# Loading one weight in five pieces to move the last store to the last semaphore of the closing list

## Chip, cores, metric

The kernel runs on one core of one Trainium2 chip. The metric is device time in microseconds (us); a median of several executions is quoted. All runs here were in the fast state with the full TensorE clock (granted clock 1.0 in every run whose clock is listed). The engines are named as in the profile: PE (TensorE; PEld is its weight loads), DVE (VectorE), ACT (ScalarE), POOL (GpSimd), SP (SyncE, which here issues every DMA).

## The reference

Two layers, each a sliding dilated attention block A and a gated MLP block B, with residuals. S = 2048 tokens, D = 1024, F = 3584, 32 heads, bfloat16.

```python
def _A_ref(x, wqkv, wo):        # q, k, v = x @ wqkv; 8 keys per token, 2 apart; softmax
    ...
    return o.reshape(B, S, D) @ wo

def _B_ref(x, w1, w3, w2):
    h = silu(x @ w1) * (x @ w3)
    return h @ w2

x = x + _A_ref(_layernorm(x), A_wqkv, A_wo)
x = x + _B_ref(_layernorm(x), B_w1, B_w3, B_w2)
x = x + _A_ref(_layernorm(x), A_wqkv, A_wo)
x = x + _B_ref(_layernorm(x), B_w1, B_w3, B_w2)
```

## The kernel before

The kernel records every operation with its reads and writes in a list, places the list with its own scheduler, and emits it in that order. The framework under it supplies the semaphores. Each DMA goes through one helper, and `wo` (2 MB) is one DMA, loaded once, in the first stage:

```python
def dma(kb, dst, src, reads, writes, cls=3, transpose=False):
    def emit(op):
        ...
        nc.sync.dma_start(dst, src)
    return pr.add("SP", 0.45, emit, reads, writes, cls, size=kb * 1024)

# ... end of q_first(), the first stage
dma(2048, wo[:], wo_v, [("d", 0, 2, 0, 6)], ["wo"], 3)

# ... t_stage(): the matmuls that use it
op = mm8(a, [(oT[oh][:, t, j * P:(j + 1) * P], wo[:, t, hh * 512:(hh + 1) * 512]) for t in range(KT)],
         True, True, [("oT", oh, t) for t in range(KT)] + ["wo"], lane=1)

# ... b_stage(): the last result leaves in small pieces
evac(dve, ..., nc.vector.tensor_tensor(xs, xs, bank[a.bank][:, 0:cn], op=ALU.add), ...)
if l == 1:
    dma(cn // 4, xout[:, n, ...], xs, [("x", n, hh)], [("out", n, hh)], 0)

# ... the emission
with tc.manual_schedule():
    for op in pr.place():
        op.emit(op)
```

The framework deals the DMAs to eight semaphores, 0 to 7, in turn. It also closes the program: SP waits for every semaphore's final value, two semaphores to an instruction, in a fixed order, and then all engines meet twice. SP's closing part, as built (numbers are DMA semaphores; DVE and ACT stand for the semaphores on which these engines report):

```
wait (3, 2)   wait (4, 1)   wait (5, 0)   wait (6, DVE)   wait (7, ACT)
drain, waits for POOL
drain, reports to POOL       wait for POOL's release     (first meeting)
drain, reports to POOL       wait for POOL's release     (second meeting)
```

Before has 468 DMAs, so the last store is on semaphore 3: the first of the five waits.

Of the kernel before, what the change touches and what calls it, by code (L numbers as in the profile page):

```python
# [154 lines left out]
def kernel(  # L155
# [15 lines left out]
    KT = D // P  # L171
# [16 lines left out]
    wo_v = A_wo.rearrange("(i t) n -> i t n", t=KT)  # L188
# [9 lines left out]
    def alloc(name, shape, dt=BF16):  # L198
        return sb.tile(shape, dt, name=name)
# [14 lines left out]
    wo = alloc("wo", [P, KT, D])  # L214
# [20 lines left out]
    oT = [alloc(f"oT{i}", [P, KT, TCH]) for i in range(2)]  # L235
# [8 lines left out]
    def t1(n):  # L244
        return 0.15 + n / 960.0
# [7 lines left out]
    def dma(kb, dst, src, reads, writes, cls=3, transpose=False):  # L253
        def emit(op):
            if transpose:
                nc.sync.dma_start_transpose(dst, src)
            else:
                nc.sync.dma_start(dst, src)  # L258
        return pr.add("SP", 0.45, emit, reads, writes, cls, size=kb * 1024)
# [77 lines left out]
    def mm8(a, pairs, first, last, reads, lane=0, ncol=512, takes=True):  # L337
        n = len(pairs)

        def emit(op):  # L340
            for i, (w, r) in enumerate(pairs):
                nc.tensor.matmul(bank[a.bank][:, 0:ncol], lhsT=w, rhs=r, start=first and i == 0,  # L342
                                 stop=last and i == n - 1)
        return pr.add("PE", n * (ncol / 2400.0 + 0.0025), emit, reads, [], takes=[a], lane=lane, lag=0.17)

    def evac(add, dur, emit, last_mm, reads, writes, a, cls=0, **kw):
        op = add(dur, emit, reads, writes, cls, gives=[a], **kw)
        op.deps.add(last_mm)
        return op
# [39 lines left out]
    def q_tile(l, c, which, ws, b, keep=None):  # L389
        for m0 in range(0, KT, 2):  # L390
            i = n_sgt[0] % 4
            n_sgt[0] += 1
            for m in (m0, m0 + 1):
                a = Acc()
                lk = [q_lhs(ws, kk, m) for kk in range(KT)]
                op = mm8(a, [(w, xnT[b][:, kk, :]) for kk, (w, _) in enumerate(lk)], True, True,
                         list({k for _, k in lk}) + [("xnT", b, j) for j in range(TPC)])
                evac(act, 0.59, lambda _, a=a, i=i, m=m: nc.scalar.copy(sgt[i][:, m % 2, :], bank[a.bank][:]), op, [],  # L398
                     [("sgt", i, m % 2)], a)
                if keep:  # L400
                    evac(act, 0.4, lambda _, a=a, m=m: nc.scalar.copy(keep[1][:, m, HALO:], bank[a.bank][:, 0:TCH]),
                         op, [], [(keep[0], m)], a)
            dma(256, spill_view(l, which, m0, c, ws[1] == "s"), sgt[i][:], [("sgt", i, 0), ("sgt", i, 1)],
                [("d", l, which, c, m0)], 1)
# [28 lines left out]
    def q_first():  # L433
# [86 lines left out]
        for which, key, tile_ in ((1, "kT", kT), (2, "vT", vT)):  # L520
            dve(0.11, lambda _, tile_=tile_: nc.vector.memset(tile_[:, :, 0:HALO], 0.0), [], [(key, "h")], 1)
            q_tile(0, 0, which, wslots[which], b, (key, tile_))
        dma(2048, wo[:], wo_v, [("d", 0, 2, 0, 6)], ["wo"], 3)
        stage_no[0] += 1

    def allkeys(key):
# [23 lines left out]
    def t_stage(l, half):  # L550
# [46 lines left out]
        oh = half % 2  # L597
# [7 lines left out]
        for j in range(TCH // P):  # L605
            n = tok0 // P + j
            for hh in range(2):
                a = Acc()
                op = mm8(a, [(oT[oh][:, t, j * P:(j + 1) * P], wo[:, t, hh * 512:(hh + 1) * 512]) for t in range(KT)],
                         True, True, [("oT", oh, t) for t in range(KT)] + ["wo"], lane=1)  # L610
                xs = x_sb[n][:, hh * 512:(hh + 1) * 512]
                evac(dve, t1(512), lambda _, xs=xs, a=a: nc.vector.tensor_tensor(xs, xs, bank[a.bank][:], op=ALU.add),  # L612
                     op, [("x", n, hh)], [("x", n, hh)], a)
# [72 lines left out]
    def attend(l, c):  # L686
        for r in range(R):
            t_stage(l, c * R + r)

    q_first()  # L690
    attend(0, 0)
    for c in range(1, NCH):
# [47 lines left out]
```

## Time and profile before

| | before |
|---|---|
| device time, first three runs | 1616.17 us median (1616.09 to 1616.46) |
| span of the profiled run | 1613.4 us |
| end of the last matmul to end of span | 2899 ns |
| issue of the last store to end of span, called **the tail** below | 2544 ns |
| SP's records in the trace | 845 |

The page shows what bounds the kernel. The rows with digits give busy tenths in 40 equal slices.

```profile
span 1613.4 us, 19212 instructions
...
PE 1608.5 (100%) x7610; PEld 762.2 (47%) x7610; DVE 1122.8 (70%) x1908; ACT 327.0 (20%) x521; POOL 5.0 (0%) x28
...
PE   9999999999999999999999999999999999999999
...
PEclk9999999999999999999999999999999999999999
```

PE is busy from end to end at full clock. The chain of work that ended last says the same in order of time. Its columns are start, length and what it was, all in us:

```profile
21 pieces in order of time: start us, us, what
...
1.66 2.78 DMA x<-in_A_x_dram
...
14.84 6.99 PE bank L504 x64
21.83 1588.68 PE bank L342 x7416
1610.51 0.02 issue
1610.54 0.29 DVE x L667
```

From 14.84 us on the chain is PE alone, for 1595.67 us. What a change can shorten without touching the matmuls is the start before that, and the end after 1610.51. The timeline of the end shows the last VectorE add, then the last store's issue on SP, and then no engine's work until 1613.4:

```profile
1610.54 0.29 DVE L667 TENSOR_TENSOR x<-x,bank 128x128 bf16<-128x128 bf16 x1 [1.28 <-PE bank L342]
1610.85 0.33 SPq L258 DMA_DIRECT2D out_dram<-x  x1
```

The waits and drains of the closing part are not counted as work and do not show there. The view of the launch line (the line of kernel.py that starts the program; the framework's closing instructions are put down to it) groups them for SP: count, duration in ns as min/median/max, first and last start in us.

```profile
L735 SPq EVENT_SEMAPHORE  x7: 17/28/28, 1612.3 to 1613.3; - x7
L735 SPq DRAIN  x3: 7/7/7, 1612.6 to 1613.0; - x3
```

One by one they are records of the trace. Below are SP's last eleven: its record number, start in ns before the end of the span, duration, and the gap since SP's record before it ended (this listing is worked out from the trace's records and is no view of the profile):

```
before
row   start   took   gap
835   -2544    332   1172   issue of the last store (semaphore 3)
836   -1069     28   1143   wait (3, 2)
837   -1005     28     36   wait (4, 1)
838    -943     28     34   wait (5, 0)
839    -879     28     36   wait (6, DVE)
840    -818     28     33   wait (7, ACT)
841    -753      7     37   drain
842    -689      7     57   drain, reports        first meeting
843    -537     17    145   wait for release
844    -445      7     75   drain, reports        second meeting
845     -63     17    375   wait for release
```

The store lands and ends the wait (3, 2) 1475 ns after its issue. The trace has the last update of semaphore 3 at 1086 ns, and the record of its wait starts 17 ns later. Four waits that were satisfied long ago are then worked off, 63 ns apart (61 to 64): 1069 - 818 = 251 ns on the critical path.

Last, the wo load before: one issue of 2 MB, 9.6 us from issue to landing.

```profile
L258 SPq DMA_DIRECT2D wo<-in_A_wo_dram x1: 497/497/497, 56.9 to 56.9; - x1
...
DMA to landing us min/median/max: 9.6/9.6/9.6
```

### The profile page before, as it was taken

To read this page: it belongs to the slowest core of one execution; us is meant where nothing else is said; L and a number is where in the kernel's file an instruction comes from. 1 tells how busy PE (TensorE), PEld (TensorE's weight loads), DVE (VectorE), ACT (ScalarE), POOL (GpSimd) and SP (SyncE) were. 2 spreads that over 40 slices of the span, in tenths; PEclk is the share of its full clock that TensorE was granted. 3 is DMA by queue.
4 is the path that set the end of the run, shared out by engine and by line. 5 is a ranking of instruction groups with operands and counts; after the bars stand their busy time and mean duration, and the time that the engine had idled before them with its cause. 6 is when DMAs were issued, how large, how long until landed. Compare 5 with 4: busy or idle time off the path is not lost.

```text
span 1613.4 us, 19212 instructions
## 1 busy us (share of the span) xinstructions
PE 1608.5 (100%) x7610; PEld 762.2 (47%) x7610; DVE 1122.8 (70%) x1908; ACT 327.0 (20%) x521; POOL 5.0 (0%) x28
## 2 busy tenths in 40 slices
PE   9999999999999999999999999999999999999999
PEld 7555544444444444444444444444444444444444
DVE  6898888889888888988888819884289831211211
ACT  4423322021201222113211032110321101101110
POOL 1000000000000000000000000000000000000000
PEclk9999999999999999999999999999999999999999
DMA  9834755485548764858554488355873464454451
GB/s 316 233 105 151 220 167 171 131 213 167 171 143 249 195 186 135 217 165 251 175 163 133 156 234 243 120 176 175 253 221 118 160 179 156 144 178 149 156 168 41
DMA packets 350073, 285.80 MB, mean 177 GB/s; under 512 B 72224, under 2 KB 344864, under 8 KB 349856
## 3 DMA queue, kind: packets, MB, share of 16 engines
q1 hardware_dynamic: 349984, 284.59, 58.7%
q8 instruction: 59, 0.97, 0.2%
q14 instruction: 30, 0.25, 0.1%
HBM read 238.94 MB, written 29.36 MB: 166 GB/s over the span
## 4 chain that ended last, share of the span: by engine, by line
PE 99%; DMA 0%; ACT 0%; SPq 0%; DVE 0%; issue 0%; ACTq 0%
PE bank L342 98%; PE bank L490 0%; PE bank L504 0%; DMA x<-in_A_x_dram 0%; PE bank L419 0%; ACT xn L453 0%; SPq L258 0%; DVE xn L457 0%; DVE x L667 0%; ACTq L453 0%
## 5 line engine op out<-in xcount | busy, mean ns | idle before, releaser
L342 PE MATMUL bank<-xnT,slot 128*128 128x512 bf16 x5056 | 1094.2, 379 | 0.0
L342 PEld LDWEIGHTS <-slot 128*128 128x128 bf16 x5056 | 517.9, 102 | 573.2
L342 PE MATMUL bank<-slot,hT 128*128 128x512 bf16 (+2 forms) x1848 | 389.2, 373 | 0.0
L637 DVE TENSOR_TENSOR hT<-sg,bank 128x512 bf16<-128x512 bf16 x224 | 153.1, 684 | 213.3 <-PE bank L342 201.5
L262 DVE TENSOR_TENSOR scr<-scr 128x1024 bf16<-128x1024 bf16 (+3 forms) x576 | 291.8, 535 | 2.0
L342 PEld LDWEIGHTS <-hT 128*128 128x128 bf16 x1848 | 178.4, 98 | 208.8
L635 ACT ACTIVATE sg<-bank 128x512 bf16<-128x512 f32 x224 | 133.7, 597 | 662.2 <-PE bank L342 624.9
L262 DVE TENSOR_TENSOR scr<-qT,kT 128x2048 bf16<-128x2048 bf16 x128 | 153.8, 1216 | 75.1 <-DMA kT<-qkv_d 73.5
L398 ACT CAST sgt<-bank 128x512 bf16<-128x512 f32 x184 | 107.4, 585 | 351.4 <-PE bank L342 348.7
L262 DVE TENSOR_TENSOR scr<-pA,vT 128x2048 bf16<-128x2048 bf16 x128 | 152.0, 1216 | 0.3
L667 DVE TENSOR_TENSOR x<-x,bank 128x512 bf16<-128x512 bf16 (+1 forms) x66 | 43.8, 670 | 123.5 <-PE bank L342 123.5
L342 PE MATMUL bank<-wo,oT 128*128 128x512 bf16 x512 | 113.1, 379 | 0.0
L309 DVE BATCH_NORM_STATS2 st<-x 128x6 f32<-128x512 bf16 x128 | 84.2, 680 | 10.7 <-DMA x<-in_A_x_dram 10.4
L342 PEld LDWEIGHTS <-oT 128*128 128x128 bf16 x512 | 50.1, 98 | 60.3
L612 DVE TENSOR_TENSOR x<-x,bank 128x512 bf16<-128x512 bf16 x64 | 43.8, 685 | 31.5 <-PE bank L342 30.5
L595 DVE STREAM_TRANSPOSE pA<-pB 128x2048 bf16<-128x2048 bf16 x16 | 37.0, 2311 | 0.5
L572 DVE STREAM_TRANSPOSE pB<-pA 128x2048 bf16<-128x2048 bf16 x16 | 37.0, 2310 | 0.4
L262 DVE TENSOR_TENSOR pA<-scr 128x256 bf16<-128x256 bf16 x128 | 35.4, 282 | 0.4
L323 DVE TENSOR_SCALAR xn<-x,mv,rstd 128x1024 bf16<-128x1024 bf16 x64 | 31.9, 540 | 4.1 <-DMA xnT<-xn 3.7
L316 ACT ACTIVATE sd<-mv,epst 128x4 f32<-128x4 f32 (+1 forms) x19 | 5.7, 299 | 142.5 <-DVE mv L312 142.3
L635 ACT ACT_TABLE_LOAD x19 | 24.4, 1283 | 48.4 <-PE bank L342 48.3
L262 DVE TENSOR_TENSOR oT<-scr 128x256 bf16<-128x256 bf16 x128 | 33.4, 282 | 0.1
(55 smaller groups left out, 203.6 us busy)
## 6 DMA issues: line engine op xcount, KB each, us to landing
slot<-in_B_w_dram SPq DMA_DIRECT2D x160, 1024.0 KB, 6.3
slot<-in_A_wqkv_dram SPq DMA_DIRECT2D x28, 1024.0 KB, 5.1
qkv_d<-sgt SPq DMA_DIRECT2D x92, 256.0 KB, 3.8
qT<-qkv_d SPq DMA_DIRECT2D x16, 512.0 KB, 4.8
slot<-in_B_w_dram SPq DMA_DIRECT2D x16, 512.0 KB, 5.8
kT<-qkv_d SPq DMA_DIRECT2D x14, 544.0 KB, 5.8
vT<-qkv_d SPq DMA_DIRECT2D x14, 544.0 KB, 5.5
out_dram<-x SPq DMA_DIRECT2D x31, 128.0 KB, 4.1
```

What stands on the lines that cost most here:

```text
L262: return lambda _: nc.vector.tensor_tensor(o, a, b, op=op)
L309: dve(0.67, lambda _, hh=hh: nc.vector.bn_stats(st[q][:, j, hh, :], x_sb[n][:, hh * 512:(hh + 1) * 512]), [("x", n, hh)] + list(after), [( ...
L316: act(0.3, lambda _: nc.scalar.activation(sd[q][:, j0:j1], mv[q][:, j0:j1, 1], ACTF.Sqrt, bias=epst[:]), [("mv", q, j) for j in range(j0, ...
L323: dve(0.5, lambda _: nc.vector.tensor_scalar(xn[j][:], x_sb[n][:], mv[q][:, j, 0:1], rstd[q][:, j:j + 1], op0=ALU.subtract, op1=ALU.mult), ...
L342: nc.tensor.matmul(bank[a.bank][:, 0:ncol], lhsT=w, rhs=r, start=first and i == 0, stop=last and i == n - 1)
L398: evac(act, 0.59, lambda _, a=a, i=i, m=m: nc.scalar.copy(sgt[i][:, m % 2, :], bank[a.bank][:]), op, [], [("sgt", i, m % 2)], a)
L572: dve(2.31, lambda _: nc.vector.transpose(psmT[:].rearrange("p c d -> p (c d)"), psm[:].rearrange("p w s -> p (w s)")), allA, ["pB"])
L595: dve(2.31, lambda _: nc.vector.transpose(At[:].rearrange("p w s -> p (w s)"), AeT[:].rearrange("p c d -> p (c d)")), ["pB"], allA)
L612: evac(dve, t1(512), lambda _, xs=xs, a=a: nc.vector.tensor_tensor(xs, xs, bank[a.bank][:], op=ALU.add), op, [("x", n, hh)], [("x", n, hh) ...
L635: evac(act, 0.6, lambda _, i=i, a=ag: nc.scalar.activation(sg[i][:], bank[a.bank][:], ACTF.Silu), og, [], [("sg", i)], ag, table="silu")
L637: evac(dve, t1(512), lambda _, i=i, a=au, f=f: nc.vector.tensor_tensor(hT[:, f, :], sg[i][:], bank[a.bank][:], op=ALU.mult), ou, [("sg", i ...
L667: evac(dve, t1(cn), lambda _, xs=xs, a=a, cn=cn: nc.vector.tensor_tensor(xs, xs, bank[a.bank][:, 0:cn], op=ALU.add), op, [("x", n, hh)], [ ...
```

## The change

The intent: four more DMAs make 472, so the last store falls on semaphore 7, whose wait is the last of the five. The four others are then worked off while the store is in flight.

```diff
-        dma(2048, wo[:], wo_v, [("d", 0, 2, 0, 6)], ["wo"], 3)
+        for t0, t1_ in ((0, 2), (2, 4), (4, 6), (6, 7), (7, 8)):
+            dma(256 * (t1_ - t0), wo[:, t0:t1_, :], wo_v[:, t0:t1_, :], [("d", 0, 2, 0, 6)], [("wo", t0)], 3)
...
-                         True, True, [("oT", oh, t) for t in range(KT)] + ["wo"], lane=1)
+                         True, True, [("oT", oh, t) for t in range(KT)] + [("wo", t) for t in (0, 2, 4, 6, 7)], lane=1)
```

## The prediction

> **What bounds the kernel now.** TensorE, from the first microseconds to the last. The page gives PE busy 1608.5 us of a 1613.4 us span, the full clock in all 40 slices, and a chain that ended last of which 98% is one matmul line. The trace's matmul records show no gap over 20 ns after 6.3 us. DVE is at 70%, ACT at 20%, the DMA queue at 58.7%. So only the two ends can become shorter: the first 6 us, and the 2.9 us from the last matmul's end (1610.50) to the end of the span.
>
> **The tail, from the trace's raw records** (ns before the end of the span). The last VectorE add starts at 2861 and takes 289; the last store is issued at 2544; its last packet starts at 1456; the wait that it ends passes at 1069. Then SyncE steps through the rest of its closing list at 63 ns each: 1005, 943, 879, 818 (four more paired waits), 753 and 689 (two drains), then two rounds of the all-engine barrier to the end. The list takes the eight DMA semaphores in fixed order, (3,2), (4,1), (5,0), (6,DVE), (7,ACT). DMAs are dealt to the semaphores in turn. Before has 468, so the last store is on semaphore 3, the first wait of the list, and four satisfied waits are worked off after the landing.
>
> **What the change does.**
> - It removes nothing and adds four DMA issues. 472 DMAs put the last store on semaphore 7, the last wait; the other four then pass while the store is in flight. Worth 1069 - 818 = 251 ns, all on the critical path. [...] here 387 ns lie between last packet and wait. That part stays.
> - The four issues cost at most 0.5 us each of SyncE (the 2 MB one takes 497 ns) near 57 us of the timeline, where SyncE mostly waits for ScalarE. The wo load lands at about 66.5 us; its first matmul is at 106.3 us. The spill buffers form a ring of four, each filled in about 3.5 us of matmuls, so a spill issued 2 us late does not reach PE.
> - Built, the programs have the same instruction order on PE, DVE, ACT and POOL and the same number of standalone waits; on SyncE only the wo pieces differ.
>
> **Prediction.** 1616.17 - 0.25 = 1615.92 us, 0.016% faster, less than the spread of the three runs (0.37 us). Eight times in ten between 1615.55 and 1616.30. Faster by over 2%: 0.003; within 2%: 0.994; slower by over 2%: 0.003.
>
> **What would show each step.** Span about 1613.15. The wait for semaphore 7 passes about 1475 ns after the last store's start, as that for semaphore 3 did; those for 3 to 6 lie before it; from it to the end 0.82 us instead of 1.07. No PE gap after 6.3 us; last matmul's end at 1610.5 within 0.05. Five wo issues, landed before 80 us.
>
> **What would make it wrong.** The last store's landing varies by over 0.25 us between runs; a wait that has blocked costs more after its release than a satisfied one; late spills near 57 us do stall PE (a gap of up to 2 us there); or the time outside the span (1.8 us in the profiled run) moves by as much.

No term of the sum is cut: it came to 1616.17 - 0.25 = 1615.92 us, and the 0.25 is the 251 ns between two starts in the listing of before. That such starts may be differenced, the prediction did not show; for the wait (3, 2) the 17 ns between the semaphore's last update and the record's start show it.

## The result, and the profile after

| | before | after |
|---|---|---|
| median | 1616.07 us (1615.23 to 1616.46, 6 runs) | 1615.88 us (1615.14 to 1616.00, 6 runs) |
| ratio of the fast runs | | 0.9999, 95% interval 0.9986 to 1.0012 |
| span of the profiled run | 1613.4 us | 1614.2 us |
| end of the last matmul | 1610.50 us | 1611.36 us |
| end of the last matmul to end of span | 2899 ns | 2808 ns |
| tail | 2544 ns | 2454 ns |
| SP's records | 845 | 849 |

A ratio here and below is the mean time of one kernel's fast runs over that of the other's of the same rounds, so not quite the ratio of the medians quoted. The median landed beside the predicted 1615.92 us. But the profile doesn't show the predicted parts. The span of this one profiled run is longer by 0.8 us, and the tail is shorter by only 90 ns instead of 251.

The 0.8 us lie at the start. The page and the chain of after:

```profile
span 1614.2 us, 19216 instructions
...
PE 1609.6 (100%) x7610; PEld 762.0 (47%) x7610; DVE 1123.4 (70%) x1908; ACT 327.1 (20%) x521; POOL 5.0 (0%) x28
...
PE   9999999999999999999999999999999999999999
```

```profile
26 pieces in order of time: start us, us, what
...
4.50 5.72 DMA slot<-in_A_wqkv_dram
...
15.70 6.99 PE bank L504 x64
22.69 1588.68 PE bank L342 x7416
1611.37 0.02 issue
1611.40 0.29 DVE x L668
```

The last 7416 matmuls take 1588.68 us in both kernels, to the hundredth. Only the point at which they begin differs, 21.83 against 22.69 us: in this run a load of the first weights landed at 10.22 us and was waited for, where before the x loads and the first transposes set the pace. The changed DMAs are issued at 57 us, so the change has no part in it. The span scatters from run to run in both kernels: after's six runs go from 1613.4 to 1614.2 us, and nine runs of before, taken later on one chip, from 1613.6 to 1614.4. The profiles put this scatter at the start: in the six that have all PE records, the row of 7416 matmuls takes 1588.68 or 1588.69 us and begins anywhere from 21.83 to 23.54 us.

The five pieces of wo were issued by 61.5 us (60.6 + 0.9) and landed within 7.6 us each:

```profile
L258 SPq DMA_DIRECT2D wo<-in_A_wo_dram x5: 339/478/882, 57.8 to 60.6; - x5
...
DMA to landing us min/median/max: 5.4/7.2/7.6
```

The end. First the view of the launch line for SP; one drain now takes 130 ns instead of 7, and the first wait starts already at 1612.1:

```profile
L736 SPq EVENT_SEMAPHORE  x7: 17/28/28, 1612.1 to 1614.1; - x7
L736 SPq DRAIN  x3: 7/7/130, 1613.2 to 1613.8; - x3
```

The same records one by one, listed as for before:

```
after
row   start   took   gap
839   -2454    332   1169   issue of the last store (semaphore 7)
840   -2076     28     46   wait (3, 2)
841   -2012     27     36   wait (4, 1)
842   -1950     28     35   wait (5, 0)
843   -1886     28     36   wait (6, DVE)
844    -996     28    862   wait (7, ACT)
845    -920      7     48   drain
846    -871      7     42   drain, reports        first meeting
847    -719     17    145   wait for release
848    -339    130    363   drain, reports        second meeting
849     -63     17    146   wait for release
```

The intended part worked. Four waits pass while the store is in flight, the wait on semaphore 7 passes 1458 ns after the issue (1475 before), and the first drain that reports comes 125 ns after it, where before it took 380. But from that drain to the end SP takes 871 ns where it took 689. The 182 ns are lost at one place: row 848 starts 363 ns after row 847 (75 ns before the change), and takes 130 ns (7 before). POOL waits for that report. Counted back from the end, its own clean-up before the second meeting was done at 409 ns, SP's report ended at 209, and POOL's wait passed at 183. Before the change SP's report had ended at 438 and POOL's clean-up at 228, so the report had about 210 ns in hand; that is why a report 411 ns late costs 182. In all the tail is 17 (the landing) + 255 - 182 = 90 ns shorter.

### What is special about row 848

In SP's records of before, a pause of 0.35 us or more stands in front of rows 80, 208, 336, 464, 592 and 720: 80 plus multiples of 128. After has it at the same row numbers, although other instructions stand there now. The gap in ns before each of these rows:

```
row        80   208   336    464   592   720   848
before    447  3250   369   5286  1156   354   (ends at row 845)
after     452   360   354  11656  5198   359   363
```

Some of these gaps include a wait. Over the ten traces there are 68 such rows, and not one gap is under 331 ns; the median gap over all other rows is about 51 ns. No other place in the count of 128 behaves so: at each of the other 127 places the shortest gap is at most 53 ns. The next in the series is 848. Before ends three records short of it. After has four records more, and so the change itself carried SP's program over it, on the last report, the last instruction but one of SP's program.

What the pause is was not shown. The page lists two queues with packets of the kind "instruction": in after 59 on queue 8, of 16384 bytes in the trace, and 31 on queue 14, of 8192. The first on queue 14 after row 847 starts 1.03 us after it (0.99 to 1.26 us in the eight profiles that reach row 848). In after that is 0.67 us after row 848 itself has started, so SP did not pause for that packet. No run here changes these packets. The pause itself and its place are measured.

### The profile page after: what moved, and what is told of

Same layout as the page of the kernel before. It is cut to its first block, busy times and chain, and to the rows that moved or that the text cites. A ratio compares the mean times of both kernels' runs of the same rounds, so it can differ in the third digit from the quotient of the medians.

```text
span 1614.2 us, 19216 instructions
## 1 busy us (share of the span) xinstructions
PE 1609.6 (100%) x7610; PEld 762.0 (47%) x7610; DVE 1123.4 (70%) x1908; ACT 327.1 (20%) x521; POOL 5.0 (0%) x28
## 4 chain that ended last, share of the span: by engine, by line
PE 99%; DMA 0%; SPq 0%; issue 0%; DVE 0%
PE bank L342 98%; PE bank L504 0%; DMA slot<-in_A_wqkv_dram 0%; PE bank L490 0%; SPq L258 0%; PE bank L419 0%; DVE x L668 0%
```

## The experiments

Theory F: a pause of about 0.3 us stands at every 128th SP record; the four added issues move it onto the closing drain, and that gives back 182 of the 251 ns. Rival C: the slow drain was an accident of one run. A second rival ties it to the split load, or to the last store being on the last semaphore. The first four kernels ran on one chip, the other four on another, each group beside nine runs of before on the same chip. Their tails were read from one profile each. In the profiles of e1 to e4 about 150 records of PE are missing; SP's are complete (row counts as built).

| run | last store on | SP rows | row 848 is | tail expected by F | tail measured | median, us | before, same chip |
|---|---|---|---|---|---|---|---|
| before | 3 | 845 | not reached | | 2544 | 1616.07 | |
| after | 7 | 849 | drain, second meeting | | 2454 | 1615.88 | 1616.07 |
| e1_after_again | 7 | 849 | drain, second meeting | 2454 | 2464 | 1615.88 | 1615.91 |
| e2_after_pad8 | 7 | 857 | first closing wait | 2272 | 2294 | 1615.85 | 1615.91 |
| e3_before_pad4 | 3 | 849 | drain, second meeting | 2726 | 2759 | 1616.23 | 1615.91 |
| e4_after_pad3 | 7 | 852 | drain right after the landing | 2580 | 2706 | 1616.21 | 1615.91 |
| e5_pieces4 | 6 | 848 | last wait of all | 2357 | 2335 | 1615.47 | 1615.93 |
| e6_pieces6 | 0 | 850 | wait, first meeting | 2420 | 2449 | 1616.01 | 1615.93 |
| e7_pieces8 | 2 | 852 | drain right after the landing | 2966 | 2998 | 1616.26 | 1615.93 |
| e8_merge4 | 7 | 838 | not reached | 2294 | 2276 | 1615.69 | 1615.93 |

All results were correct, and every time ratio to before lies between 0.9998 and 1.0002 with an interval of about 0.13% on either side, so no single time proves a difference. The tails do: the only program profiled twice (after, and e1) differs by 10 ns, and the part of the tail that hangs on the store's landing, from the last store's issue to the pass of its wait, lies between 1458 and 1478 ns in the eight profiles where the record shows it directly (all but e6 and e7).

### e1_after_again

Edit: none.

> The changed kernel, unaltered, to see what repeats. Tail = from the issue of the last store to the end of the span: 2544 ns before, 2454 ns after, in the two profiles so far. Theory F [...]: SyncE pauses about 0.31 us at every 128th of its instructions; the four added DMA issues put such a pause on its second closing drain (row 848 of 849), which gives back 182 of the 251 ns. Then the tail repeats: 2454 +- 40 ns, with about 360 ns before row 848. Rival C (chance): the slow drain was an accident of one run; then the tail is about 2290 ns. Time: 1615.9 us for F, 1615.8 for C; the start of the kernel scatters by about 0.8 us in either.

Measured: tail 2464 ns, with gap 363 and 130 ns for row 848 again, to the nanosecond as in after. Rival C falls.

### e2_after_pad8

Empty drains on SP, in mid-kernel where SP mostly waits for other engines (984 us of before's span for PE alone), are there only to shift row numbers:

```diff
+n_sp = 0
 for op in pr.place():
     op.emit(op)
+    if op.eng == "SP":
+        n_sp += 1
+        if n_sp == 300:
+            for _ in range(8):
+                nc.sync.drain(fusable=False)
```

> After, with 8 empty drains on SyncE in mid-kernel: same DMAs, same semaphores, 857 SyncE rows, so row 848 becomes the first of the closing waits, which is passed while the last store is still in flight. F: the pause is hidden, tail 2272 +- 40 ns (251 + about 20 below before), median about 1615.7 us. Rival C or a rival that ties the slow drain to the split load or to the last semaphore: tail as in after, 2454 ns.

Measured: tail 2294 ns, 160 to 170 ns below after's two profiles. The view of the launch line shows the drain short again:

```profile
L742 SPq EVENT_SEMAPHORE  x7: 17/28/28, 1611.7 to 1613.2; - x7
L742 SPq DRAIN  x3: 7/7/7, 1612.6 to 1612.9; - x3
```

The pause is still there, 343 ns in front of row 848, but that row is now the first closing wait, and the store is still in flight. From the wait on semaphore 7 to the end it takes 818 ns, exactly as from the same wait in before. So 251 ns is what the semaphore's place is worth when nothing takes it back.

### e3_before_pad4

Edit: the same insertion with 4 drains, in the kernel before (one wo load, last store on semaphore 3).

> Before, with 4 empty drains on SyncE in mid-kernel: one wo load, last store on semaphore 3, but 849 SyncE rows as in after. F: row 848 is again the second closing drain; tail 2544 + 182 = 2726 +- 40 ns, median about 1616.25 us. Rivals (chance, split load, last semaphore): 2544 ns, 1616.07 us.

Measured: tail 2759 ns, 215 above before.

```profile
L741 SPq EVENT_SEMAPHORE  x7: 17/28/28, 1613.2 to 1614.4; - x7
L741 SPq DRAIN  x3: 7/7/116, 1613.5 to 1614.1; - x3
```

The slow drain appears without a split load and without the last semaphore, by the row count alone (gap 382, 116 ns). This disposes of the second rival.

### e4_after_pad3

Edit: the same insertion with 3 drains, in after.

> After, with 3 empty drains: 852 rows, so row 848 is the drain that directly follows the wait for the last store. F: the pause lies wholly on the critical path: tail 2272 + 310 = 2580 +- 50 ns, worse than before's 2544 although the last store is on the last semaphore; median about 1616.0 us. Rivals: 2454 ns (split load or last semaphore), 2290 ns (chance).

Measured: tail 2706 ns, so worse than before, as F said, but by more than its 2580 ± 50.

```profile
L742 SPq EVENT_SEMAPHORE  x7: 17/28/28, 1612.1 to 1614.4; - x7
L742 SPq DRAIN  x3: 7/7/130, 1613.6 to 1614.0; - x3
```

The size was off, not the place. I had taken the pause as the gap alone, 0.31 us. Where row 848 is a drain, the drain itself also takes 130 ns instead of 7. From the wait on semaphore 7 to the report it takes 551 ns here (1240 - 689) and 129 in e2 (818 - 689), so the pause costs 422 ns where nothing hides it. The expectations of the next group use that.

### e5_pieces4

```diff
-for t0, t1_ in ((0, 2), (2, 4), (4, 6), (6, 7), (7, 8)):
+for t0, t1_ in ((0, 2), (2, 4), (4, 6), (6, 8)):
```

with the list of keys that the matmuls read changed alike (so also in the next two).

> After, with wo in four pieces instead of five: 471 DMAs, last store on semaphore 6, so one satisfied wait is left behind it (63 ns); 848 SyncE rows, so the pause falls before the very last wait, in front of which SyncE idles 375 ns anyway. F: tail 2294 + 63 = 2357 +- 40 ns, about 100 ns below the five pieces although the last store is not on the last semaphore. If only the semaphore's place counted: 63 ns above the five pieces, 2525 ns. Median about 1615.8 us.

Measured: tail 2335 ns, below after's although the last store is not on the last semaphore. Row 848 is the very last wait; its gap is 376 ns, as it was at that place in before without any pause (375), so the pause hides there for free.

### e6_pieces6

```diff
-for t0, t1_ in ((0, 2), (2, 4), (4, 6), (6, 7), (7, 8)):
+for t0, t1_ in ((0, 2), (2, 4), (4, 5), (5, 6), (6, 7), (7, 8)):
```

> wo in six pieces: 473 DMAs, last store on semaphore 0, two satisfied waits behind it (126 ns); 850 rows, row 848 is SyncE's wait for the first barrier's release. There SyncE idles 145 ns, so it is late by about 210 ns, within the about 230 ns that the second drain has in hand (its 411 ns delay in after cost 182). F: tail 2294 + 126 = 2420 +- 50 ns. If only the semaphore's place counted: 126 ns above the five pieces, 2590 ns.

Measured: tail 2449 ns. The wait at row 848 came 374 ns after the row before it instead of 145, and most of that was absorbed by the slack of the second meeting: the tail is 29 ns above the 2420 that two satisfied waits alone give. The median was above before's although the tail is shorter by 95 ns; the profiled run began its long row of matmuls at 23.54 us, 1.71 us later than that of before, so this run carries the start's scatter.

### e7_pieces8

```diff
-for t0, t1_ in ((0, 2), (2, 4), (4, 6), (6, 7), (7, 8)):
+for t0, t1_ in ((0, 1), (1, 2), (2, 3), (3, 4), (4, 5), (5, 6), (6, 7), (7, 8)):
```

> wo in eight pieces: 475 DMAs, last store on semaphore 2, in the first closing wait as in before, so no gain from the semaphore; 852 rows, so row 848 is the drain behind the wait for the last store, which cost 422 ns in full with the three pads. F: tail 2544 + 422 = 2966 +- 50 ns, the slowest of all, median about 1616.45 us. If only the semaphore's place counted: 2544 ns, as before.

Measured: tail 2998 ns, the longest of all, 454 above before, at a place in the closing list that is no worse than before's.

```profile
L736 SPq EVENT_SEMAPHORE  x7: 17/28/1112, 1611.9 to 1614.4; - x7
L736 SPq DRAIN  x3: 7/7/130, 1613.6 to 1614.0; - x3
```

A side finding sits in the first line. The wait (3, 2) has a record of 1112 ns here. Semaphore 2, the one it truly waited for, is the second of its pair. Where the one waited for is the first of the pair (all other profiles), the waiting lies in the gap and the record takes 28 ns. In e6, where it is the second again (semaphore 0 in the pair (5, 0)), the record takes 989 ns.

### e8_merge4

The other direction: four DMAs fewer than before instead of four more.

```diff
-        for kk in range(3, KT):
+        for kk in range(3, KT - 2):
             rows[2](kk)
+        i1 = rows[0][1]
+        v1 = slot[i1][:].rearrange("p (k c) -> p k c", k=4)
+        dma(512, v1[:, 2:4, :], wqkv_v[:, 6:8, 0:D], [], [("w", i1, 2), ("w", i1, 3)], 0)
...
-        for m0 in range(0, KT, 2):
-            dma(256, spill_view(0, 0, m0, 0), hT[:, m0:m0 + 2, :], ...)
+        dma(1024, qkv_d[0][0].rearrange("(m p) s -> p m s", p=P)[:, :, 0:CH], hT[:, 0:KT, :], ...)
```

> The kernel before with four DMAs fewer instead of four more: the four spills of the first q tile as one, and the last two row loads of the first weights as one. 464 DMAs, last store on semaphore 7, 838 SyncE rows: row 848 is never reached. F: tail 2294 +- 40 ns, as with eight pads, with no padding; median about 1615.7 us if the merged loads do not hurt the start. If the gain needed the split wo: 2544 ns.

Measured: tail 2276 ns, the shortest of all; median 1615.69 us beside 1615.93 for before. The last store is on semaphore 7, and SP ends ten rows short of 848. The gain needs neither the split load nor padding.

```profile
L737 SPq EVENT_SEMAPHORE  x7: 17/28/28, 1612.0 to 1613.8; - x7
L737 SPq DRAIN  x3: 7/7/7, 1613.1 to 1613.5; - x3
```

### Do the times follow?

As far as they can. The mean of each kernel's runs less the mean of before's on the same chip, beside the difference of the tails, in us: e1 +0.01 and -0.08; e2 -0.11 and -0.25; e3 +0.35 and +0.22; e4 +0.22 and +0.16; e5 -0.43 and -0.21; e6 +0.18 and -0.10; e7 +0.33 and +0.45; e8 -0.22 and -0.27. The three kernels with a lengthened tail are all slower, and each of the eight lies within 0.3 us of its tail, which is what five runs with a start that scatters by 0.8 us allow. None of these differences clears its interval.

## Why the prediction was right or wrong

- **PE bounds the kernel, and only the ends can become shorter: right.** The chain's last 7416 matmuls take 1588.68 us before and after.
- **The last store moves to semaphore 7 and four waits pass during its flight: right.** The wait passed 1458 ns after the store's issue (predicted 1475), and the report to POOL came 255 ns sooner after it (380 to 125; predicted 251). e2 shows 251 exactly when it stands alone. The starts could be differenced here: in after too the wait's record starts 17 ns after the semaphore's last update (1013 to 996), and takes 28 ns. In e6 and e7, where the semaphore waited for is the second of its pair, the waiting lies inside the record (989 and 1112 ns), and its start would not do.
- **"It removes nothing and adds four DMA issues ... Worth 1069 - 818 = 251 ns, all on the critical path": the step that failed.** The sum left out a term. I costed the four issues where they stand, at 57 us, and took them as free; I did not cost what four more instructions do to the place of all later ones. They carried a pause that stands at every 128th SP record onto the last drain. It gave back 182 ns, measured in the profile and reproduced by e1 (182) and e3 (187), so the tail became 90 ns shorter instead of 251 (the landing came 17 ns earlier). "0.82 us instead of 1.07" from the last wait to the end was 0.996. The periodic pause was there to be seen in the trace before; I had looked only at the last microseconds.
- **The four issues do no harm near 57 us: right in effect, one size off.** I said at most 0.5 us each; one took 0.88. SP does mostly wait for ACT there: in before, between 50 and 75 us, 11.9 us for ACT and 4.6 for PE and DVE. No PE gap over 20 ns appears there in after, and the loads land some 40 us before their first use at 107 us.
- **Span about 1613.15, last matmul's end at 1610.5 within 0.05, no PE gap after 6.3 us: wrong.** They were 1614.17, 1611.36, and gaps at 6.9, 8.2 and 10.2 us (277, 26 and 52 ns). I took the start of one profiled run as fixed, but the span scatters by 0.8 us in either kernel, and the profiles put that at the start.
- **1615.92 us, between 1615.55 and 1616.30: the median of 1615.88 is inside.** That agreement is luck, and no evidence for 251 ns: the real difference of the tails, 0.09 us, lies as well inside the scatter, and so would no difference at all.

What stays open: what makes the start scatter, and what the pause is.

## What to carry to other kernels

An instruction added far from the critical path still moves every later one on its queue (here four DMA issues added near 57 us turned 845 SP records into 849, and put a closing drain on row 848); when a gain is no larger than the pause cost here (182 to 422 ns), check what periodic pause now falls on the closing instructions, by listing the gaps of that queue by record number. Judge such a gain by the tail in single records, which repeated within 10 ns in the one pair here, and not by the time, which scattered by 0.8 us. If the last store is to sit on the last semaphore waited for, both directions are open, and what decides is where the pause then falls: taking four DMAs away made the tail 268 ns shorter (e8, which ends before row 848), adding four 90 ns (after). Fewer instructions are no safer in themselves: e4 has five SP records fewer than e2, and its tail is 412 ns longer.
